# Where the second MLP's weight pairs are emitted beside the attention, and what their column sums are ordered behind

## The chip, the core and the metric

The kernel runs on one core of a Trainium2 chip. The metric is the time of one execution on the device, in microseconds (us), as the median of several runs. Beside it stands one execution recorded by the hardware profiler, whose trace gives every duration below.

Engines are named as the profile names them: PE is TensorE (matmuls), PEld its weight loads, DVE is VectorE, ACT is ScalarE, POOL is GpSimd, SP is SyncE, which issues nearly all DMAs here. Each engine works through its own list of instructions. A scheduler writes these lists when the program is built.

## The reference

```python
def _attn_ref(q, k, v, w1, b1, w2):                    # (4, 8, 576, 64) each
    scores = scale * np.matmul(q, k.transpose(0, 1, 3, 2))
    ...                                                # a bias per head from a small MLP on relative positions
    attn = np.exp(scores - max) / (sum + 1e-09)
    return np.matmul(attn, v)

def _moe_ref(x, w1, w2, w3, w_out):                    # first MLP: 2304 x 512, d_ff 768
    h = np.maximum(np.maximum(x @ w1, x @ w2), x @ w3)
    return h @ w_out

def _moe2_ref(x, w_in, w_out):                         # second MLP: 2304 x 512, d_ff 2048
    h = x @ w_in
    g = np.where(h >= 1, h, np.where(h <= -1, 0.0, (h + 1) ** 2 / 4))
    return g @ w_out
```

Attention, then the first MLP, then the second. Matrices are multiplied in two float16 parts, a high one and a low one, so each product takes three matmuls. Before a weight is split into these parts it is scaled by a power of two that is taken from the sums of its columns' sizes.

## The kernel before

**Attention.** The queries are cut into blocks `j` of 128 rows (and a last one of 64, `SJ`), and the work into slots: one slot is one head, or pair of heads, of one block and batch. The loop over `i` (line 939) emits, for slot `i`, its scores for the next slot, its softmax, side work, and the multiplication with V (`emit_pv`, 14 matmuls of 128x64, line 753, or 28 of line 749) of the slot three before. The first MLP's matmuls (line 808 with the three input weights, line 830 with the output weights) come from a queue `mlp_q`: some run beside the attention, and what is left is drained after the last slot by a loop over `mlp_q`.

**Weights of the second MLP.** `late_pieces` brings them in 16 pairs of 128 rows or columns of `w_in` and `w_out`. For a pair two raw tiles are loaded by SP (line 450) into buffers named `v` or `ws`. ACT and DVE decode them (lines 462, 463, 464, 465), then `pair_scale` takes the column sums: eight matmuls with a matrix of ones on PE (line 549, result in a PSUM tile `pm` or `s`), a maximum on DVE (line 552) and three small steps to the scale (lines 136, 137, 141), and ACT and DVE write the high and the low half (lines 157 and 158). `late_to(n)` emits pieces up to a number. In the attention's last blocks (`u.j >= 3`) it stops at `N_BIAS` = 10 pieces, that is five pairs; the other eleven pairs are emitted in the loop that drains `mlp_q`.

**The drain.** In it PE does the first MLP's matmuls of the last two groups of tokens, whose operands are named `masks` and `xT`, and the column sums of the eleven pairs. ACT decodes and splits weights, and takes the MLP's results out of PSUM (lines 813 and 835). DVE does its half of both.

**The second MLP, first block.** Per step `ft` PE multiplies with `w_in` (line 1056), ACT and DVE form the activation (ACT 1069, DVE 1070 and 1071, ACT 1073, DVE 1074), and PE multiplies with `w_out` two steps later (line 1082). Between these steps `wcomb(q)` is emitted eight times: POOL forms sums and differences of the weights that later blocks need (lines 1120 to 1124), ACT writes their high half (line 1125) and POOL the low one (line 1126). The other blocks (lines 1134 and 1173 on PE) follow.

**What sets the order.** The build's scheduler picks instructions by their priority and by a timeline of its own; `tc.issue_after(x)` keeps what is emitted inside it behind instruction `x` in the order. Without it an instruction can be put anywhere that its operands allow. So a small change in what is emitted when can reshuffle the lists further on.

Of the kernel before, what the change touches and what calls it, by code (L numbers as in the profile page):

```python
# [20 lines left out]
def kernel(ctx: ExitStack, tc: tile.TileContext, qt, kt, vr, small, mw1, mw2, mw3, mwo, win, wo2, out):  # L21
# [7 lines left out]
    V, A, G, T, SP = nc.vector, nc.scalar, nc.gpsimd, nc.tensor, nc.sync  # L29
    P = 128  # L30
# [46 lines left out]
    @contextmanager  # L77
    def sooner(what):

        n = PRM["po"].get(what, 0)  # L80
        n = min(n, tc.cur_priority)
        tc.cur_priority -= n
        yield
        tc.cur_priority += n
# [79 lines left out]
    if True:  # L164
# [303 lines left out]
        def high(y):  # L468

            return y.bitcast(BF16)[:, 0:512]  # L470
# [67 lines left out]
        def late_to(n):  # L538
            while n_late[0] < n:
                n_late[0] += 1  # L540
                next(late)

        def pair_scale(s, ys, k):

            pn = mlp_ps()
            for i, y in enumerate(ys):
                yb = high(y)
                for kk in range(KK):
                    T.matmul(pn[:, P * i:P * i + P], ones, yb[:, P * kk:P * kk + P], start=(kk == 0), stop=(kk == KK - 1))
            n = s.shape[1]  # L550
            t = st([P, 2], F32, "tcol2")[:, :n]
            V.tensor_reduce(t, pn[:, :2 * P].rearrange("p (n c) -> p n c", n=n), AX.X, ALU.max)
            floor2(t, t)
            inv2(s, t, k)
# [144 lines left out]
        def halves(t):  # L699
            return t.rearrange("p (a c) -> p a c", a=2)  # L700

        last_soft, last_turn = [None], [None]

        def emit_soft(i):
            u, s = slots[i]
# [32 lines left out]
        def emit_pv(i):  # L738
            u, s = slots[i]
            if s == 0:  # L740
                u.pav = ps.tile([P, 512], F32, tag="pav", name="pav", bufs=1)
            pt = ptbox.pop(i)
            for x, (c, sl) in enumerate(PVSEQ):
                kw = dict(start=(x == 0), stop=(x == len(PVSEQ) - 1))
                if u.j == SJ:
                    for r in range(2):
                        h = PAIRS[s][r]
                        v = kbox[("v", 3, u.b, h // 4)]
                        T.matmul(u.pav[64 * r:64 * r + 64, 64 * s:64 * s + 64], pt[:, c, 64 * r:64 * r + 64], v[:, sl, 64 * (h % 4):64 * (h % 4) + 64], **kw)
                else:  # L750
                    v = kbox[("v", u.j, u.b, s // 4)]
                    h = HEADS[s]
                    T.matmul(u.pav[:, 64 * h:64 * h + 64], pt[:, c], v[:, sl, 64 * (h % 4):64 * (h % 4) + 64], **kw)  # L753
            return s == u.n - 1

        xbox = {}
# [182 lines left out]
        for i in range(NS + LAG + 1):  # L939
            if i == NS:  # L940
                wide.append(1)
            if i < NS:
                u, s = slots[i]
                at = i - start_of[u.j]
                if at == 0 and u.j < 3:
                    with behind(i):
                        xts[u.j + 1] = xtable(u.j + 1)
                    bias_q.extend((u.j + 1, gq) for gq in range(18))
                    if u.j == 2:
                        xts[SJ] = xtable(SJ)  # L950
                        bias_q.extend((SJ, gq) for gq in range(9))
                with sooner("att"):
                    prefetch(i + PRM["ahead"])
                    prefetch_v(i)
                    emit_s(i + 1)
                    emit_soft(i)
            with sooner("norm"):
                while pend_norm:
                    emit_norm(pend_norm.pop(0))
            if i < NS:  # L960
                with sooner("v"):
                    if PRM["ef"]:
                        for f, *a in early.get(i, ()):
                            with behind(i), tc.issue_after(last_score[0].ins) if f is v_max else tc.issue_after(last_turn[0].ins) if f is v_store else nullcontext():
                                f(*a)
                with sooner("w"):
                    while conv_left and PRM["cm"][6 - len(conv_left)] <= i:
                        with behind(i):
                            conv_moe(conv_left.pop(0))
                b_at, b_n = PRM["bias"][min(u.j, 2)]  # L970
                with sooner("bias"):
                    for _ in range(rate("bias", (27 if u.j == 2 else 18) / b_n) if at >= b_at and not conv_left else 0):
                        if bias_q:
                            a = bias_q.pop(0)
                            a = (*a, new_xt(a[0]))
                            if a[0] == SJ:
                                bias_short(*a)
                            else:
                                bias_group(*a, B1[cnt["b"] % len(B1)])
                                cnt["b"] += 1  # L980
                with sooner("v"):
                    if not PRM["ef"]:
                        for f, *a in early.get(i, ()):
                            f(*a)
                if i >= (WO if n_wo[0] >= NF1 else PRM["woz"]):
                    with sooner("wo"):
                        for _ in range(rate("conv", PRM["c0"] if n_wo[0] < NF1 else PRM["c1"])):
                            if n_wo[0] != NF1 or i >= WO:
                                n_wo[0] += 1
                                next(pieces, None)  # L990
                with sooner("mlp"):
                    for _ in range(rate("mlp", PRM["mlp"][u.j])):
                        e = next_mlp(i >= WO and (wo_done or not PRM["ww"]))
                        if e:
                            e[0](*e[1])
            if i < NS and u.j >= 3:
                with sooner("late"), tc.issue_after(last_soft[0].ins):
                    late_to(min(N_BIAS, n_late[0] + rate("late", PRM["late"][0])))
            if i >= LAG and i - LAG < NS:
                with sooner("att"):  # L1000
                    last_pv = emit_pv(i - LAG)
                if last_pv:
                    uu = slots[i - LAG][0]
                    pend_norm.append(uu)
                    key = (uu.j, uu.b // 2 if uu.j != SJ else 0)
                    half = 4 * uu.j + uu.b < PRM["half"]
                    if half or uu.b == B - 1 or (uu.j != SJ and uu.b == 1):
                        done_blocks.append((i, key, slice(128 * (uu.b % 2), 128 * (uu.b % 2) + 128) if half else slice(0, 256)))
            while done_blocks and i >= done_blocks[0][0] + 2:
                queue_mlp(*done_blocks.pop(0)[1:])  # L1010
# [262 lines left out]
```

## Time and profile before

| | |
|---|---|
| median of 3 runs | 1004.85 us (1003.17, 1004.85, 1009.06) |
| profiled execution | 1001.5 us, span 999.6 us |
| PE busy | 927.2 us, 93% of the span |
| DVE, ACT, POOL busy | 689.0, 599.2, 514.1 us |
| mean granted TensorE clock | 0.96 of full speed |

The profiled execution has a time of its own, 1001.5 us; its span goes from the first to the last instruction. Busy times are sums over the whole span, so they hide that different stretches have different limits.

In the rows below a time is in us from the span's start, then comes the duration of a group, then engine, line, operation and operands (`out<-in`). What stands in square brackets is how long the engine had been idle before it, and whose end ended that.

### The profile page before, as it was taken

The numbers are of one execution on the slowest core, as the hardware profiler recorded it, in microseconds if no ns is written. First come the engines' busy times: TensorE is split into PE (matmuls) and PEld (weight loads), VectorE is DVE, ScalarE is ACT, GpSimd is POOL, SyncE is SP. The second block draws the span as 40 slices with busy tenths as digits, with TensorE's granted clock in tenths as the row PEclk, the third lists the DMA queues.
The fourth block names the chain that finished last, engine by engine and source line by source line (L and its number), as shares of the span: only waits on it lengthen the run. The fifth ranks groups of instructions, "written<-read, shape, count | busy, mean of one in ns | idle before, by whom it ended". The sixth has DMA issues, their size and how long they took to land. (4 is left out here: it accounts for less than half of the span.)

```text
span 999.6 us, 25925 instructions
## 1 busy us (share of the span) xinstructions
PE 927.2 (93%) x10258; PEld 756.0 (76%) x10258; DVE 689.0 (69%) x1512; ACT 599.2 (60%) x1194; POOL 514.1 (51%) x734
## 2 busy tenths in 40 slices
PE   6768988899999999999899899999999999999996
PEld 5546777688888878778678778543688888888885
DVE  8998886767656686566454577876477586686565
ACT  3789875856665645778577698633444454454442
POOL 4133496748767755646367103995143344343442
PEclk8777979899999999999999999999999999999999
DMA  9996997997999879999989663010110010000000
GB/s 289 266 261 161 271 220 210 232 247 168 218 237 206 178 178 212 218 230 225 216 172 210 193 202 106 22 43 1 43 44 23 1 43 23 2 22 23 1 23 22
DMA packets 238969, 141.46 MB, mean 142 GB/s; under 512 B 187520, under 2 KB 217728, under 8 KB 238336
## 3 DMA queue, kind: packets, MB, share of 16 engines
q1 hardware_dynamic: 238688, 139.55, 58.6%
q8 instruction: 80, 1.31, 0.5%
q14 instruction: 41, 0.34, 0.1%
q10 hardware_dynamic: 160, 0.26, 0.1%
HBM read 79.68 MB, written 15.27 MB: 95 GB/s over the span
## 5 line engine op out<-in xcount | busy, mean ns | idle before, releaser
L808 PEld LDWEIGHTS <-aw 128*128 128x128 f16 x2160 | 190.1, 99 | 42.5 <-issue 20.0
L808 PE MATMUL pm<-xT,aw 128*128 128x256 f16 (+1 forms) x1812 | 201.9, 264 | 4.4 <-ACT hl L835 2.0
L731 POOL TENSOR_TENSOR phl<-sp,phl 128x512 f16<-128x512 f32 x136 | 162.2, 1193 | 0.0
L713 ACT ACTIVATE sp<-sp,mx 128x576 f32<-128x576 f32 x144 | 110.6, 769 | 67.8 <-DVE mx L711 67.3
L730 POOL TENSOR_TENSOR phl<-sp,phl 128x64 f16<-128x64 f32 x136 | 49.0, 360 | 189.6 <-ACT phl L729 157.1
L697 PE MATMUL s<-k,qz 64*128 64x288 f32 (+1 forms) x576 | 127.1, 459 | 15.1 <-DVE mx L711 9.8
L711 DVE CUSTOM_DVE_ANT_0 sp<-s,ab 128x576 f32<-128x576 f32 x128 | 93.2, 751 | 28.0 <-PE s L697 13.8
L1151 ACT ACTIVATE sp<-pm,vec 128x256 f32<-128x256 f32 x112 | 61.3, 555 | 80.0 <-PE pm L1134 77.2
L697 PEld LDWEIGHTS s<-k,qz 64*128 64x128 f32 (+1 forms) x576 | 69.0, 199 | 33.7 <-DVE mx L711 12.5
L729 ACT ACTIVATE phl<-sp 128x576 f16<-128x576 f32 x136 | 90.0, 673 | 4.8 <-DMA pt<-phl 4.1
L753 PEld LDWEIGHTS <-pt 128*128 128x128 f16 x1792 | 72.3, 100 | 25.5 <-DMA pt<-phl 14.4
L1155 POOL TENSOR_TENSOR hh<-hh 128x128 f32<-128x128 f32 x56 | 32.9, 588 | 106.4 <-DVE hh L1153 90.3
L1134 PEld LDWEIGHTS <-ab 128*128 128x128 f16 x756 | 73.8, 98 | 9.2
L753 PE MATMUL pav<-v,pt 128*128 128x64 f16 x1568 | 69.2, 195 | 9.0 <-DMA pt<-phl 8.9
L1152 DVE SCALAR_TENSOR_TENSOR hh<-pm,vec,sp 128x256 f32<-128x256 f32 x112 | 52.4, 477 | 32.3 <-ACT sp L1151 32.0
L820 POOL TENSOR_TENSOR hh<-hm,hh 128x256 f16<-128x256 f32 (+1 forms) x60 | 45.9, 766 | 52.4 <-ACT hh L819 52.3
L830 PE MATMUL pm<-hh,wo 128*128 128x256 f16 x558 | 70.3, 276 | 1.7 <-ACT hh L819 0.9
L830 PEld LDWEIGHTS <-wo 128*128 128x128 f16 x648 | 61.6, 99 | 13.1 <-issue 5.0
L815 DVE SCALAR_TENSOR_TENSOR hm<-pm,hm 128x256 f32<-128x256 f32 (+1 forms) x108 | 42.0, 389 | 33.7 <-PE pm L808 16.3
L1173 PEld LDWEIGHTS <-xT 128*128 128x128 f16 x588 | 57.4, 98 | 7.8 <-ACT xT L1160 1.2
L1173 PEld LDWEIGHTS <-wo 128*128 128x128 f16 x588 | 57.5, 98 | 6.7
L1156 POOL TENSOR_TENSOR hh<-hh 128x128 f32<-128x128 f32 x56 | 26.2, 468 | 68.4 <-DVE hh L1153 66.2
(298 smaller groups left out, 1986.1 us busy)
## 6 DMA issues: line engine op xcount, KB each, us to landing
k<-in_k_dram SPq DMA_DIRECT2D x64, 288.0 KB, 4.0
v<-v_d SPq DMA_DIRECT2D x24, 640.0 KB, 5.0
ws<-in_moe_w_out_dram SPq DMA_DIRECT2D x15, 512.0 KB, 5.1
ws<-in_moe_w_in_dram SPq DMA_DIRECT2D x9, 512.0 KB, 5.9
x_d<-hl SPq DMA_DIRECT2D x36, 128.0 KB, 2.6
qz<-in_q_dram SPq DMA_DIRECT2D x16, 256.0 KB, 4.4
ab<-in_moe_w_dram SPq DMA_DIRECT2D x8, 512.0 KB, 8.6
qz<-x_d SPq DMA_DIRECT2D x4, 1024.0 KB, 4.8
```

The lines of the kernel that those rows point to most:

```text
L697: last_score[0] = T.matmul(sbox[i + r][:, c, :288], q[p, s if u.j == SJ else s // 2], k[p, 288 * c:288 * c + 288], start=True, stop=True)
L711: last_pair[0] = V.tensor_tensor_reduce(halves(sn), sbox.pop(i)[:, :, :288], halves(bias_sb[u.j][:, h]), -0.125, 3e38, ALU.add, ALU.min, mx)
L713: last_soft[0] = A.activation(pf, sn, AF.Exp, scale=-1.0, bias=mx, accum_out=u.sums[:, h:h + 1])
L729: A.activation(hl[:, :S], pf, AF.Copy)
L731: G.tensor_tensor(hl[:, S + 64:], pf[:, :512], hl[:, :512], ALU.subtract)
L753: T.matmul(u.pav[:, 64 * h:64 * h + 64], pt[:, c], v[:, sl, 64 * (h % 4):64 * (h % 4) + 64], **kw)
L808: T.matmul(o, wm[:, ft, i, wp, kk], x_rhs(key, xp, kk) if n == 256 else x_rhs(key, xp, kk)[:, c], start=(x == 0), stop=(x == 11))
L830: T.matmul(pm, wo16[:, ft, wp, P * d:P * d + P], hh[:, ft, hp], start=(ft == 0 and y == 0), stop=(ft == NF1 - 1 and y == 2))
L1134: T.matmul(pm, w[:, wp, kk], x2t[ORDER[y]][:, kk, xp, 256 * sub:256 * sub + 256], start=(x == 0), stop=(x == 11))
L1151: A.activation(r, pm, AF.Relu, scale=c_ch[:, f], bias=c_half)
L1152: V.scalar_tensor_tensor(t, pm, c_c[:, f], r, ALU.mult, ALU.max)
L1173: T.matmul(m[x], gl[:, gp, i], w[:, wp], start=(start and z == 0 and x % 2 == 0), stop=(stop and z == 2 and (x % 2 == 1 or x == 6)))
```

## The change

The call of `late_to` inside the attention moves: it stood ahead of `emit_pv`, and stands behind it now. It is under the same condition and with the same number, as `i >= LAG` always holds there. And the eight column-sum matmuls of each pair are put into `tc.issue_after(last_mm)`, where `last_mm` is the last multiplication with V that was emitted. The softmax order that it was under (`last_soft`) stays. After the attention `last_mm` remains the very last multiplication with V, so the column sums of the drain's eleven pairs are ordered behind that one too.

```diff
@@ pair_scale
             pn = mlp_ps()
-            for i, y in enumerate(ys):
-                yb = high(y)
-                for kk in range(KK):
-                    T.matmul(pn[:, P * i:P * i + P], ones, yb[:, P * kk:P * kk + P], start=(kk == 0), stop=(kk == KK - 1))
+            with tc.issue_after(last_mm[0].ins) if last_mm else nullcontext():
+                for i, y in enumerate(ys):
+                    yb = high(y)
+                    for kk in range(KK):
+                        T.matmul(pn[:, P * i:P * i + P], ones, yb[:, P * kk:P * kk + P], start=(kk == 0), stop=(kk == KK - 1))
@@ emit_pv (both matmuls)
-                    T.matmul(u.pav[:, 64 * h:64 * h + 64], pt[:, c], ...)
+                    last_mm[:] = [T.matmul(u.pav[:, 64 * h:64 * h + 64], pt[:, c], ...)]
@@ the slot loop
-            if i < NS and u.j >= 3:
-                with sooner("late"), tc.issue_after(last_soft[0].ins):
-                    late_to(min(N_BIAS, n_late[0] + rate("late", PRM["late"][0])))
             if i >= LAG and i - LAG < NS:
                 with sooner("att"):
                     last_pv = emit_pv(i - LAG)
+                if i < NS and u.j >= 3:
+                    with tc.issue_after(last_soft[0].ins):
+                        late_to(min(N_BIAS, n_late[0] + rate("late", PRM["late"][0])))
```

The diff adds one line, so from `pair_scale` on most line numbers of the changed kernel are one higher: its column sums are line 550, the multiplication with V 754, the first MLP 809, its evictions 814 and 836, `wcomb`'s ACT step 1126.

In the built programs the lists of all five engines have the same instructions in the same order, line numbers aside, up to the last slot of the attention. The five pairs beside the attention stand where they stood. The first place that differs is on PE, in the last slot: the column sums of the first pair of the drain (operands `xtab` and `ab`) beside the last 14 multiplications with V. Before:

```order
L808 MATMUL s<-masks,aw 128x256
L549 LDWEIGHTS ones
L549 MATMUL s<-xtab,ones 128x128
L549 LDWEIGHTS ones
L549 MATMUL s<-xtab,ones 128x128
L753 LDWEIGHTS pt
L753 MATMUL pav<-v,pt 128x64
```

And the same place in the changed kernel:

```order
L809 MATMUL s<-masks,aw 128x256
L809 LDWEIGHTS aw
L809 MATMUL pm<-masks,aw 128x256
L754 LDWEIGHTS pt
L754 MATMUL pav<-v,pt 128x64
...
L550 LDWEIGHTS ones
L550 MATMUL s<-xtab,ones 128x128
```

Two of the eight column sums stood ahead of the 14 multiplications and six behind; now all eight stand behind, and two first-MLP matmuls have moved ahead in their place.

Further on, in the drain, ACT's list is dealt out differently. The names: `hl` is the first MLP's output taken out of PSUM (tiles `pm`, `s`), `masks`, `ws` and `ab` are places of weights. Before, in the middle of the drain:

```order
L835 ACTIVATE hl<-pm,vec 128x64 x4
L835 ACTIVATE hl<-s,vec 128x64 x4
L462 ACTIVATE sp<-v 128x512
L463 ACTIVATE ws<-ws 128x512
L462 ACTIVATE sp<-ws 128x512
L463 ACTIVATE ws<-v 128x512
L835 ACTIVATE hl<-pm,vec 128x64 x4
L465 ACTIVATE ws<-sp 128x512
L835 ACTIVATE hl<-pm,vec 128x64 x2
L157 ACTIVATE masks<-sp,vec 128x512 x2
L835 ACTIVATE hl<-pm,vec 128x64 x2
```

Now:

```order
L462 ACTIVATE sp<-v 128x512
L836 ACTIVATE hl<-pm,vec 128x64 x4
L836 ACTIVATE hl<-s,vec 128x64 x4
L463 ACTIVATE ws<-v 128x512
L465 ACTIVATE ws<-sp 128x512
L462 ACTIVATE sp<-ws 128x512
L463 ACTIVATE ws<-ws 128x512
L157 ACTIVATE masks<-sp,vec 128x512 x2
L463 ACTIVATE ws<-v 128x512
L836 ACTIVATE hl<-pm,vec 128x64 x4
L814 ACTIVATE hm<-s 128x256
L836 ACTIVATE hl<-pm,vec 128x64 x4
```

The third and the fourth eviction of the group (`hl<-pm`) now stand behind more weight work: one L465, the two L157 and one L463 have moved ahead of the third.

The last place is ACT's list at the start of the second MLP. Before:

```order
L1125 ACTIVATE aw<-xT 128x1024
L835 ACTIVATE hl<-s,vec 128x128 x2
L1069 ACTIVATE sp<-pm,vec 128x512
L1073 ACTIVATE phl<-sp,vec 128x512
L1069 ACTIVATE sp<-pm,vec 128x512
L1125 ACTIVATE aw<-xT 128x1024
L835 ACTIVATE hl<-s,vec 128x128 x2
L835 ACTIVATE hl<-pm,vec 128x128 x2
L1073 ACTIVATE phl<-sp,vec 128x512
L1069 ACTIVATE sp<-pm,vec 128x512
```

Now:

```order
L1126 ACTIVATE aw<-xT 128x1024
L836 ACTIVATE hl<-s,vec 128x128 x2
L1070 ACTIVATE sp<-pm,vec 128x512
L1074 ACTIVATE phl<-sp,vec 128x512
L1126 ACTIVATE aw<-xT 128x1024
L836 ACTIVATE hl<-s,vec 128x128 x2
L836 ACTIVATE hl<-pm,vec 128x128 x2
L1070 ACTIVATE sp<-pm,vec 128x512
L836 ACTIVATE hl<-s,vec 128x128 x2
L1070 ACTIVATE sp<-pm,vec 128x512
L1074 ACTIVATE phl<-sp,vec 128x512 x2
L1126 ACTIVATE aw<-xT 128x1024
```

The second activation step (the second L1069, now L1070) stood ahead of the second `wcomb` step and stands behind it. Further on three more pairs of neighbours change places: the fourth L1069 stood ahead of the third `wcomb` step and stands behind it, the eighth L1069 stood ahead of the sixth `wcomb` step and stands behind it, and the ninth L1073 stood ahead of the seventh and stands behind it. The eighth and last `wcomb` step stands between the tenth L1073 and the eleventh L1069 in both.

## Rows read from the trace of the kernel before

**Rows 1.** Busy us (and instructions) of each engine by stretch; clock, DMA share, GB/s

```profile
0.00:545.00 545.00, 492.10 (x6578) 405.22 (x6579) 383.88 (x914) 372.50 (x816) 321.07 (x441) 0.93 0.96 219
545.00:632.00 87.00, 79.17 (x784) 67.91 (x782) 57.88 (x142) 67.05 (x141) 21.33 (x24) 1.00 0.52 162
632.00:693.00 61.00, 57.42 (x273) 25.94 (x272) 43.78 (x46) 26.14 (x39) 56.65 (x47) 1.00 0.07 24
693.00:962.00 269.00, 269.00 (x2363) 230.97 (x2364) 184.07 (x376) 122.30 (x184) 103.76 (x201) 1.00 0.06 22
```

**Rows 2.** The chain that ended last, around the start of the second MLP

```profile
622.61 2.70 DVE k L158 x2
...
628.68 2.42 POOL aw L1126
...
688.53 0.77 ACT sp L1069
...
692.17 0.76 DVE phl L1074
692.98 2.33 PE s L1082 x10
```

**Rows 3.** PE in order of time, in the drain

```profile
572.76 0.38 PE L549 MATMUL pm<-ab,ones 128*128 128x128 bf16 x4 [1.30 <-ACT ab L465]
...
595.56 1.47 PE L808 MATMUL pm<-xT,aw 128*128 128x256 f16 x12
598.06 1.47 PE L808 MATMUL pm<-xT,aw 128*128 128x256 f16 x12 [1.03 <-ACT hl L835]
...
607.48 2.78 PE L808 MATMUL s<-xT,aw 128*128 128x256 f16 x24 [1.81 <-ACT hm L813]
```

**Rows 4.** ACT in order of time, drain and start of the second MLP

```profile
574.93 0.68 ACT L463 ACTIVATE ab<-v 128x512 uint32<-128x512 uint32 x1 [1.71 <-DMA v<-in_moe_w_out_dram]
...
594.51 0.94 ACT L835 ACTIVATE hl<-pm,vec 128x64 f32<-128x64 f32 x4
...
596.21 1.39 ACT L157 ACTIVATE masks<-sp,vec 128x512 f16<-128x512 f32 x2
...
604.44 0.67 ACT L463 ACTIVATE k<-v 128x512 uint32<-128x512 uint32 x1 [0.91 <-DMA v<-in_moe_w_out_dram]
...
632.32 0.76 ACT L1069 ACTIVATE sp<-pm,vec 128x512 f32<-128x512 f32 x1
...
637.80 0.63 ACT L835 ACTIVATE hl<-pm,vec 128x128 f32<-128x128 f32 x2
...
644.87 1.06 ACT L1125 ACTIVATE aw<-xT 128x1024 f16<-128x1024 f32 x1 [2.11 <-POOL xT L1124]
...
671.98 1.06 ACT L1125 ACTIVATE aw<-xT 128x1024 f16<-128x1024 f32 x1 [3.71 <-POOL xT L1124]
...
680.50 1.06 ACT L1125 ACTIVATE aw<-xT 128x1024 f16<-128x1024 f32 x1 [2.11 <-POOL xT L1124]
```

**Rows 5.** PE in order of time, first block of the second MLP

```profile
638.84 1.89 PE L1082 MATMUL s<-ab,phl 128*128 128x512 f16 x8
...
669.18 2.33 PE L1082 MATMUL s<-ab,phl 128*128 128x512 f16 x10 [0.70 <-DVE phl L1074]
...
675.87 2.33 PE L1082 MATMUL s<-ab,phl 128*128 128x512 f16 x10 [1.34 <-DVE phl L1074]
...
680.63 2.75 PE L1082 MATMUL s<-ab,phl 128*128 128x512 f16 x12
...
692.19 0.60 PE L1082 MATMUL s<-ws,phl 128*128 128x512 f16 x2 [1.04 <-ACT phl L1073]
```

**Rows 6.** POOL in order of time, `wcomb`: one step in two lengths

```profile
632.20 0.73 POOL L1122 TENSOR_TENSOR xT<-xT 128x256 f32<-128x256 f32 x1
...
667.40 1.17 POOL L1122 TENSOR_TENSOR xT<-xT 128x256 f32<-128x256 f32 x1
```

**Rows 7.** DVE in order of time, the same stretch: L1074 beside POOL

```profile
655.43 2.46 DVE L1074 SCALAR_TENSOR_TENSOR phl<-sp,vec,phl 128x512 f16<-128x512 f32 x1 [1.19 <-ACT phl L1073]
```

More of the change, by code (lines that the diff above doesn't have):

```diff
@@ L700, in halves @@
             return t.rearrange("p (a c) -> p a c", a=2)
-        last_soft, last_turn = [None], [None]
+        last_soft, last_turn, last_mm = [None], [None], []
         def emit_soft(i):
@@ L748, in emit_pv @@
                         v = kbox[("v", 3, u.b, h // 4)]
-                        T.matmul(u.pav[64 * r:64 * r + 64, 64 * s:64 * s + 64], pt[:, c, 64 * r:64 * r + 64], v[:, sl, 64 * (h % 4):64 * (h % 4) + 64], **kw)
+                        last_mm[:] = [T.matmul(u.pav[64 * r:64 * r + 64, 64 * s:64 * s + 64], pt[:, c, 64 * r:64 * r + 64], v[:, sl, 64 * (h % 4):64 * (h % 4) + 64], **kw)]
                 else:
@@ L752, in emit_pv @@
                     h = HEADS[s]
-                    T.matmul(u.pav[:, 64 * h:64 * h + 64], pt[:, c], v[:, sl, 64 * (h % 4):64 * (h % 4) + 64], **kw)
+                    last_mm[:] = [T.matmul(u.pav[:, 64 * h:64 * h + 64], pt[:, c], v[:, sl, 64 * (h % 4):64 * (h % 4) + 64], **kw)]
             return s == u.n - 1
```

## The prediction

> **What bounds the kernel now.** I read the busy times by stretch first, then the chain of waits, then PE and ACT in order of time where the chain changes engine.
>
> The stretches [rows 1] tell where a change could matter at all. From 693 to 962 us PE is busy 269.00 of 269.00 us. Nothing that only moves instructions can shorten that. From 545 to 632, the drain of the first MLP, PE is busy 79.17 of 87.00 us and ACT 67.05. From 632 to 693, the first block of the second MLP, PE is busy 57.42 of 61.00 us and POOL 56.65. So PE is idle 7.83 us in the drain and 3.58 us in the block behind it, 11.41 us together. The granted clock is 1.00 in all three stretches, the full 2.4 GHz level, although PE waits in two of them, so I count no clock loss and no gain.
>
> The chain [rows 2] says which engine sets the end of the second stretch. It runs through DVE's last weight pairs (622.61), then along POOL's `wcomb` from 628.68 to the eighth step, then to ACT's L1069 at 688.53, DVE's L1074 at 692.17 and PE's L1082 at 692.98, and from there along PE to the end. So the end comes when POOL's chain and what is behind it is through, and PE has some room until then: its waits at 669.18, 675.87 and 692.19 [rows 5].
>
> **The attention: 0.** No instruction is added or removed. The five pairs beside the attention are the first 10 of 32 pieces. On all five lists they stand where they stood, so emitting them later in the slot, and behind the multiplication with V, changes nothing in the first 545 us [rows 1]. With equal lists the waits are equal too. What is left is the drain and the block behind it.
>
> **The last slot: 0.** Two column sums move behind the 14 multiplications with V. These are eight short matmuls; four of them take 0.38 us as a group [rows 3]. Nobody waits for them there: the next steps of that pair on DVE stand behind a decode step that waits for a DMA.
>
> **The drain, ACT's first part: 0, from -1.3 to 0.** An eviction and a decode step change places around 562 us. Whatever PE gains there it loses at 572.76, where it waits 1.30 us for ACT's L465 [rows 3], which is as late as before, since the same ACT steps stand in front of it. If ACT came earlier by all of that wait, 1.30 us would be won.
>
> **The drain, the first MLP's evictions: 0, up to +1.5.** The third eviction of the group, at 594.51 before, now has one L465, two L157 and one L463 more in front of it. By rows the two L157 take 1.39 us and an L463 0.67 [rows 4]; taking the same for an L465 this makes 2.7 us, so the eviction starts at about 597.2 and ends at 598.1 with its 0.94. PE's twelve matmuls that ran at 595.56 need its PSUM buffer [rows 3]. They come 2.5 us late. The wait of 1.03 us at 598.06 for the fourth eviction then falls away, because the fourth now follows directly and PE arrives later: 1.5 us are left. At 607.48 PE waited 1.81 us for ACT [rows 3], and that swallows the 1.5. I take 0, and keep +1.5 for the case that the ACT step waited for there comes later as well.
>
> **The drain, the loads: 0, from -2.6 to +0.7.** SP's list differs in a handful of loads of weights that move by a place ahead of or behind stores of the first MLP's output. ACT waited 1.71 us for a landing at 574.93 and 0.91 at 604.44 [rows 4], together 2.62. Where ACT frees raw buffers earlier, the next load starts earlier. Around 604 I read a gain of some 0.6 from the order: two L462 that free raw tiles stand earlier by about that. But soon behind it the two L157 of another pair, which took 1.39 in the row above, have moved behind an L463 that waits for a load, so that ACT waits with work left to do, and gives it back. Hence 0.
>
> **The start of POOL's chain: 0.** The gate is the last pair's scale, behind DVE's two L158 at 622.61 [rows 2]; the order around it on DVE, and the L157 and the first L1125 on ACT behind it, are as before but for one L819.
>
> **The first block of the second MLP: +1.2.** Here ACT's list puts activation steps behind `wcomb` steps that wait for POOL. Four cases:
>
> - The second L1069 was at 632.32. Now it is behind the second L1125 and four evictions, which ended at 637.80 + 0.63 = 638.4 [rows 4]. From an L1069 to its L1074's end it takes 4.4 us on the chain (688.53 to 692.93) [rows 2], and one more activation step of about 0.8 stands between now: ready at 643.6. PE's second L1082 group would start after the first one, which began at 638.84 [rows 5] and takes 2.6, at about 641.5. PE is 2 us late, and its later waits of 0.70 and 1.34 [rows 5] swallow that.
> - The third L1125, at 644.87 [rows 4], now follows the third L1073. The second step's result is there at 643.6, and about 2 us of DVE's and ACT's work for the third follow: 645.6, which is 0.7 later. POOL had other work in most of that time, so I let its chain lose 0.2.
> - The eighth L1069 now stands behind the sixth L1125, which ends at 671.98 + 1.06 = 673.0 [rows 4]. With 4.4 us its result is there at 677.4. PE took it up at 675.87 [rows 5]: +1.5.
> - The ninth L1073 stands behind the seventh L1125, so it starts at 680.50 + 1.06 = 681.6 [rows 4], and with L1073 and L1074 of about 0.75 each the result is there at 683.1. PE began that group at 680.63 [rows 5], and would now begin at 682.1, so it loses another 0.9: +2.4 in all.
>
> At 692.19 PE waited 1.04 and then 0.18 us more, until 692.98, for the eleventh step [rows 2, 5], which still depends on POOL's eighth `wcomb`. That swallows 1.2 of the 2.4. So +1.2 is left, and POOL's 0.2 lies beside it. From 693 on PE has no idle time, so +1.2 goes to the end in full. Bounds: 0, if the waits are dealt out more kindly, and +2.4.
>
> One more price in this stretch is POOL's. Its L1122 takes 0.73 us at 632.20 and 1.17 at 667.40 [rows 6], and DVE's L1074, 0.76 on the chain at 692.17 [rows 2], takes 2.46 us at 655.43 [rows 7], next to POOL. So the two engines hold each other up when they meet, and the change moves DVE's steps against POOL's. I take 0 for it, as the number of meetings is about the same.
>
> **Sum.** 0 + 0 + 0 + 0 + 0 + 1.2 = +1.2 us on the profiled execution's own time of 1001.5, that is 1002.7. That execution is 3.35 us below the median of the three runs (1004.85), which themselves range over 5.9 us. The mean of all four executions is 1004.6. I put the sum on that: 1004.6 + 1.2 = 1005.8.
>
> **Rivals.**
>
> 1. *The drain gets shorter.* If earlier freed raw buffers take both waits for landings (1.71 + 0.91) from ACT [rows 4] and PE follows, POOL's chain starts 2.6 us earlier and PE's losses behind it stay: 1004.6 - 2.6 + 1.2 = 1003.2; without those losses 1002.0. For a gain of over 5 us nearly half of the 11.41 us would have to go. For it speaks that ACT has little other idle time in the drain; against it that the order gives back at the next pair what it wins.
> 2. *POOL's chain gets longer* (slower). If the activation's DVE steps now meet `wcomb` at other points, each of eight L1122 could take 1.17 in place of 0.73, which is +3.5, and the 1.2 of PE's waits turn into POOL's. From the point where the eighth L1125 ends later than before, each microsecond goes straight to the end, as PE waits for it at 692.19. With the late third L1125 and the +1.5 of the evictions: 1004.6 + 3.5 + 0.2 + 1.5 = 1009.8.
>    The Trainium skill's page "SBUF — State Buffer", section "SBUF: two separate sides", says that VectorE and GpSimd share one pair of ports as an exclusive lock, and that the one which comes second waits for the other's whole instruction. By that rule, the trace agrees: 2.46 is 0.76 and most of another engine's instruction. A `wcomb` step could then lose a whole 0.76 per meeting, eight times 6.1, and the sum would be 1010.7.
> 3. *The change does what its words say in the attention after all*, that is the same lists run in another rhythm. Then the five pairs' forty column sums come later, at 0.38 us per four: 3.8 us of PE work shifted, of which the end would see at most 3.8 in either direction, 1000.8 or 1008.4. Against it speaks that nothing on the lists differs.
>
> **How the numbers follow.** Forecast 0.66, rival 1 0.16, rival 2 0.14, rival 3 0.04. The forecast's own range is 1003 to 1008: its bounds 0 to +2.4 and half of the scatter of the runs. With rivals 1 and 2 and half of the scatter below the former's 1002.0 to 1003.2 the range is 1000 to 1010. What differs by less than 0.5%, 5 us, a measurement of this kernel can't tell from no change. Over 5 us faster needs rival 1 with more than its waits, 0.06 of its 0.16, and 0.02 from the forecast and rival 3: 0.08. Slower by over 5 us is over half of rival 2 (0.08) and a little of the forecast and rival 3 (0.02): 0.10. Same is the rest: 0.82.
>
> **What would show it right or wrong.** In the new profile: the attention up to the last slot with the times of before to a few tenths; a PE wait near 595 that is longer, and the one near 607 shorter or gone; the eighth `wcomb` step on ACT near 688; waits of PE for L1074's results near 642, 676 and 682, and none or a short one at 692. The idle time of PE between 545 and 693 should be 12 to 14 us where it was 11.41. I am wrong if the eighth `wcomb` step comes more than 2 us earlier or later, or if the attention's times move.

## The result, and the profile after

The changed kernel takes 1012.73 us in the median of 11 runs (1010.16 to 1018.76), the kernel before 1007.84 in 11 runs beside it (1002.31 to 1009.93). The ratio is 1.0065, with a 95% interval of 1.0046 to 1.0085. So the change makes the kernel slower by 0.65%; the medians lie 4.9 us apart, the means 6.6. I had forecast no measurable change, 1005.8 us in a range of 1000 to 1010: the forecast was wrong.

The profiled execution took 1011.35 us, with a span of 1009.6. First its busy times by stretch, in the columns of [rows 1]:

```profile
0.00:545.00 545.00, 488.56 (x6551) 402.05 (x6552) 379.62 (x911) 369.01 (x811) 319.97 (x438) 0.93 0.97 217
545.00:632.00 87.00, 75.86 (x785) 66.91 (x782) 55.88 (x132) 66.38 (x139) 18.20 (x25) 1.00 0.56 170
632.00:693.00 61.00, 55.34 (x258) 25.20 (x257) 44.82 (x56) 26.07 (x40) 56.06 (x46) 0.97 0.08 27
693.00:962.00 269.00, 269.00 (x2321) 226.66 (x2319) 181.42 (x366) 121.11 (x181) 103.06 (x197) 1.00 0.06 21
```

PE's idle time from 545 to 693 is 11.14 + 5.66 = 16.80 us, where it was 11.41. I had expected 12 to 14. The granted clock, 1.00 before, is 0.97 in the third stretch.

The two profiles can't be laid on each other as they are. The last multiplication with V begins at 554.89 us before and at 557.63 after, though the instructions ahead of it are the same; over the 13 profiles of this study that I could use it lies between 554.89 and 565.41. So I take its start as the zero, and compare what comes behind, which I call the tail. First before, then after:

```profile
554.89 0.57 PE L753 MATMUL pav<-v,pt 128*128 128x64 f16 x14
```

```profile
557.63 0.57 PE L754 MATMUL pav<-v,pt 128*128 128x64 f16 x14
```

By that measure the kernel before ends at 999.6 - 554.89 = 444.7 us and the changed one at 1009.6 - 557.63 = 452.0: 7.3 more.

PE in order of time, answering to [rows 3, 5]:

```profile
595.71 1.47 PE L809 MATMUL pm<-xT,aw 128*128 128x256 f16 x12 [0.32 <-ACT hl L836]
...
601.94 1.47 PE L809 MATMUL pm<-xT,aw 128*128 128x256 f16 x12 [2.14 <-ACT hl L836]
...
612.17 2.78 PE L809 MATMUL s<-xT,aw 128*128 128x256 f16 x24 [1.31 <-ACT hm L814]
...
645.42 2.02 PE L1083 MATMUL s<-ab,phl 128*128 128x512 f16 x6 [2.90 <-ACT hl L836]
647.24 3.91 PE L1057 MATMUL pm<-ws,ab 128*128 128x512 f16 x12
...
692.20 2.33 PE L1083 MATMUL s<-ab,phl 128*128 128x512 f16 x10 [1.35 <-DVE phl L1075]
```

The wait for the third eviction is there, 2.14 us. The matmuls of 595.56 in [rows 3] are at 601.94, and with 2.74 us taken off for the zero that is 3.6 later. The wait of 1.03 is gone, but that of 1.81 us [rows 3] has only fallen to 1.31, so 612.17 - 607.48 - 2.74 = 1.95 us of lateness pass it. The first L1083 is 3.8 us late, behind a wait of 2.90, and the twelve L1057 behind it take 3.91 us, where twelve matmuls of that size took 2.75 before [rows 5]: the clock has fallen after the wait. From 646 to 648 us the granted clock is 0.54, from 648 to 650 it is 0.61.

The chain of waits, answering to [rows 2]. It runs along POOL again, then DVE and PE:

```profile
636.89 2.15 POOL aw L1127
...
687.11 1.18 POOL xT L1125
690.01 2.14 DVE phl L1075
692.20 2.33 PE s L1083 x10
```

And ACT's steps in it, first those of the kernel before, the first and the eighth:

```profile
627.56 1.04 ACT L1125 ACTIVATE aw<-xT 128x1024 f16<-128x1024 f32 x1
...
687.57 1.06 ACT L1125 ACTIVATE wo<-xT 128x1024 f16<-128x1024 f32 x1 [2.48 <-POOL xT L1124]
```

Then the changed kernel:

```profile
634.53 1.33 ACT L157 ACTIVATE k<-sp,vec 128x512 f16<-128x512 f32 x2 [4.92 <-DVE vec L141]
635.77 1.04 ACT L1126 ACTIVATE aw<-xT 128x1024 f16<-128x1024 f32 x1
...
688.31 1.06 ACT L1126 ACTIVATE aw<-xT 128x1024 f16<-128x1024 f32 x1 [3.26 <-POOL xT L1125]
689.27 0.70 ACT L1074 ACTIVATE phl<-sp,vec 128x512 f16<-128x512 f32 x1
...
695.40 1.06 ACT L1126 ACTIVATE wo<-xT 128x1024 f16<-128x1024 f32 x1 [0.67 <-POOL xT L1125]
```

ACT stood 4.92 us in front of the last pair's L157, waiting for its scale from DVE. The first `wcomb` step follows at 635.77. It was at 627.56, so with 2.74 taken off for the zero it is 8.2 - 2.74 = 5.5 us late. The eighth, at 695.40, was at 687.57: 5.1 late. The chain is thus not longer than before, it starts later. And PE's last wait now ends behind the seventh step (688.31), not the eighth.

### The profile page after: what moved, and what is told of

It is laid out like the page before. It is cut to its first block, busy times and chain, and to the rows that moved or that the text cites. A ratio compares the mean times of both kernels' runs of the same rounds, so it can differ in the third digit from the quotient of the medians.

```text
span 1009.6 us, 25929 instructions
## 1 busy us (share of the span) xinstructions
PE 927.8 (92%) x10258; PEld 755.3 (75%) x10258; DVE 689.0 (68%) x1512; ACT 599.0 (59%) x1194; POOL 512.9 (51%) x734
## 3 DMA queue, kind: packets, MB, share of 16 engines
q8 instruction: 80, 1.31, 0.5%
## 5 line engine op out<-in xcount | busy, mean ns | idle before, releaser
L714 ACT ACTIVATE sp<-sp,mx 128x576 f32<-128x576 f32 x144 | 110.5, 768 | 66.7 <-DVE mx L712 66.3
```

Of the source, the lines that this page charges most:

```text
L714: last_soft[0] = A.activation(pf, sn, AF.Exp, scale=-1.0, bias=mx, accum_out=u.sums[:, h:h + 1])
```

## Experiments

For all profiles this table has the start of the last multiplication with V, and counted from there the first `wcomb` step on ACT (in e5, e6, e10 and e11 it isn't on ACT), the eighth low half on POOL (L1126 before), and the span's end, that is the tail; the last column is the end less the eighth step.

| kernel | last V | first step | eighth | end | end - eighth |
|---|---|---|---|---|---|
| before | 554.89 | 72.7 | 133.8 | 444.7 | 310.9 |
| e1 changed, drain not ordered | 560.00 | 74.3 | 135.1 | 446.0 | 310.9 |
| e4 before, scales behind | 565.41 | 73.0 | 134.7 | 445.6 | 310.9 |
| changed | 557.63 | 78.1 | 138.9 | 452.0 | 313.1 |
| e2 order alone | 561.85 | 77.4 | 138.1 | 451.3 | 313.1 |
| e3 changed, scales behind | 560.56 | 75.6 | 136.4 | 449.4 | 313.0 |
| e9 changed, eviction first | 561.26 | 76.9 | 138.4 | 449.5 | 311.1 |
| e8 both | 562.00 | 73.5 | 135.1 | 446.2 | 311.1 |
| e12 both, again | 562.58 | 74.5 | 136.1 | 447.3 | 311.2 |
| e5 before, copies on POOL | 560.79 | - | - | 440.7 | - |
| e11 the same, again | 562.94 | - | - | 441.4 | - |
| e6 changed, copies on POOL | 560.06 | - | - | 444.8 | - |
| e10 the same, eviction first | 556.82 | - | - | 443.5 | - |

### Which part of the change it is: e1 and e2

```diff
 e1 (changed kernel)
         fetch_x2(0)
+        last_mm.clear()
         for x, (f, a) in enumerate(mlp_q):
```

e2 is the kernel before with `issue_after(last_mm)` around the column sums, and `late_to` left where it was. Line numbers aside, e1's lists of all five engines are those of the kernel before, and e2's are those of the changed one.

> The changed kernel in full, except that the column sums of the drain's pairs are no longer ordered behind anything: the note of the last matmul with V is forgotten before the first MLP is drained. The pairs emitted in the attention keep both parts of the change. Theory (only the drain's first pair has its sums moved, and all that was lost follows from that): the time of the kernel before, ratio 0.998 to 1.002, with POOL's first L1127 near 629 us and last L1083 near 721 us. Rival A (the sums ordered behind the matmuls with V, or the pairs emitted at the end of a slot, cost time inside the attention): stays near the changed kernel, ratio 1.004 to 1.009, and the first column sum near 409 us again.

> The ordering alone: the pairs are emitted where the kernel before emits them, but every pair's column sums are ordered behind the last matmul with V. Theory: the changed kernel's time, ratio 1.005 to 1.009, first L1126 of POOL's chain about 5 us later than before when the last matmul with V is taken as the zero. Rival A (the position of the pairs' emission costs): between the two kernels, ratio 1.001 to 1.004.

e1: ratio 1.0016 (0.9992 to 1.0040). e2: 1.0065 (1.0040 to 1.0089). So the position of the pairs beside the attention costs nothing, and neither does their order there, nor the `sooner("late")` that the moved call lost. The whole loss comes from the drain, and there from the first pair's sums, two of which moved behind 14 multiplications with V: with the order on that pair alone the lists are those of the changed kernel, too, and with it on every pair but that one they are those of the kernel before. The absolute times that I wrote for e1 were missed, because its attention was 5 us slower; in the table it stands with the kernel before.

### VectorE's scale steps: e3 and e4

```diff
                     if ft % GROUP == 0:
-                        scales(0, slice(ft, ft + GROUP), ft // GROUP)
+                        with tc.issue_after(last_split[0].ins):      # the last pair's L158
+                            scales(0, slice(ft, ft + GROUP), ft // GROUP)
```

In the changed kernel, as in the kernel before, DVE's list has four scale steps for the second MLP between the second last pair's scale (L141) and its split (L158). In the changed kernel:

```profile
627.75 0.44 DVE L141 TENSOR_SCALAR vec<-tcol 128x2 uint32<-128x2 uint32 x1
628.22 0.65 DVE L1033 TENSOR_SCALAR vec<-vec 128x16 f32<-128x16 f32 x1
628.91 0.60 DVE L141 TENSOR_SCALAR vec<-vec 128x16 uint32<-128x16 uint32 x1
629.54 1.07 DVE L1035 TENSOR_SCALAR vec<-vec 128x16 f32<-128x16 f32 x1
630.53 0.77 DVE L1036 TENSOR_SCALAR vec<-vec 128x16 f32<-128x16 f32 x1
631.22 2.30 DVE L158 SCALAR_TENSOR_TENSOR k<-sp,vec,k 128x512 f16<-128x512 f32 x2
```

Before, with the same four steps between them:

```profile
620.39 0.15 DVE L141 TENSOR_SCALAR vec<-tcol 128x2 uint32<-128x2 uint32 x1
...
622.52 2.78 DVE L158 SCALAR_TENSOR_TENSOR k<-sp,vec,k 128x512 f16<-128x512 f32 x2
```

The last pair's scale is behind all of them. The edit changes DVE's list alone.

> The changed kernel, with DVE's scale steps of the second MLP's first block (four rows of VectorE's list) put behind the split of the last pair of weights; no other engine's list differs. Theory (the last pair's scale waits on VectorE behind these steps, which take about 3 us beside POOL's first group, and POOL's chain of L1126 and L1127 follows one to one): the split of the last pair 2 to 3 us earlier, first L1126 and the end 2 to 3 us earlier, ratio 1.002 to 1.006 to the kernel before. Rival B (the chain of wcomb groups does not set the end; TensorE's matmuls in the drain do): the split comes earlier, the end does not move, ratio 1.005 to 1.009. Rival C (the scale steps are then late for the first group of the second MLP): the end moves by less than 1 us or gets later.

> The kernel before with the same edit of VectorE's list alone. Theory: there the last pair's scale is held by these steps for about 1 us, so the split comes up to 1 us earlier and the end with it, ratio 0.998 to 1.0. Rival B: nothing moves, ratio 0.999 to 1.001. Rival C: the scale steps are late for the first group, ratio 1.001 to 1.003.

e3: ratio 1.0036 (1.0012 to 1.0060). DVE, with the steps behind the last pair's split:

```profile
630.11 0.44 DVE L141 TENSOR_SCALAR vec<-tcol 128x2 uint32<-128x2 uint32 x1
631.40 2.55 DVE L158 SCALAR_TENSOR_TENSOR k<-sp,vec,k 128x512 f16<-128x512 f32 x2 [0.85 <-ACT k L157]
...
635.72 1.41 DVE L158 SCALAR_TENSOR_TENSOR k<-sp,vec,k 128x512 f16<-128x512 f32 x2 [0.87 <-ACT k L157]
...
637.52 1.98 DVE L1037 TENSOR_SCALAR vec<-vec 128x16 f32<-128x16 f32 x1
```

From L141 to the first L158 it takes 1.29 us where it took 3.47. In the table the first step of the chain is 1.8 to 2.5 us earlier than in the two profiles of the changed lists, and the end 1.8 to 2.5 earlier. That is the theory, at the lower end of the size expected, and it speaks against rival B, though the interval of the ratio still overlaps that of the change. It doesn't make these steps the cause of the loss. They stand in the same place in the kernel before, where L141 to L158 took 2.13 us, and in e1, which has that kernel's lists, 3.77, more than the changed kernel's 3.47. So e3 takes out a price that both kernels pay.

e4: ratio 1.0035 (1.0009 to 1.0060), above all that I wrote, rival C's 1.001 to 1.003 included. But the profile doesn't show rival C: the end is 445.6 us behind the last V, as in the other two kernels with the lists of before, so in the tail nothing moved (rival B). There the split did come earlier, but ACT then waited 0.84 us for POOL's own sums:

```profile
636.26 1.33 ACT L157 ACTIVATE k<-sp,vec 128x512 f16<-128x512 f32 x2 [2.26 <-DVE vec L141]
638.43 1.06 ACT L1127 ACTIVATE aw<-xT 128x1024 f16<-128x1024 f32 x1 [0.84 <-POOL xT L1126]
```

What is late next took the place of the wait. In this profile what e4 loses lies ahead of the last multiplication with V, which began at 565.41; the last section comes back to it.

### Does POOL's chain carry the loss to the end: e5, e6 and e11

```diff
-            A.activation(t_home[q][:, 0], t, AF.Copy)      # ACT, L1125
+            G.tensor_copy(t_home[q][:, 0], t)              # POOL
```

The lists differ from those of the two kernels only from the first such copy on.

> The kernel before, with the eight copies of POOL's chain (ScalarE's L1125, float32 to float16) done on POOL itself, so that ScalarE's list holds no step that waits for POOL between the steps that release TensorE. The chain gets longer by what eight such copies take on POOL, but the first reader of its result is the second block. Theory (the chain sets the end because its steps stand in ScalarE's list): the waits of TensorE in the first block (1.34 us at 675.87, 1.04 us at 692.19) go, the end comes 2 to 4 us earlier, ratio 0.996 to 0.998. Rival B (TensorE's own work and its waits in the drain set the end): nothing moves, 0.999 to 1.001. Rival C (POOL, fuller by the copies, slows VectorE's steps or is late for the second block): slower, 1.002 to 1.01.

> The changed kernel with the same edit. Theory: here the chain starts about 5 us later and holds TensorE longer, so the edit gives back more, 5 to 7 us; what is left against the same edit of the kernel before is TensorE's own lateness in the drain, 2 to 3 us. Ratio to the kernel before 0.998 to 1.001. Rival B: ratio stays at 1.005 to 1.009, and the difference to the other kernel with this edit stays 5 to 7 us. Rival C: slower than the changed kernel.

> The kernel before with the copies on POOL, the fastest so far, beside the same kernel's runs once more. Theory (the chain's steps in ScalarE's list cost the kernel before its two waits in the first block, 3.5 us in all): ratio 0.996 to 0.999. Rival (that gain is lost to POOL and VectorE in each other's way): 1.0 to 1.002.

e5: 0.9991 (0.9971 to 1.0011), and measured again as e11 0.9946 (0.9923 to 0.9969). e6: 0.9995 (0.9973 to 1.0017), where the changed kernel had 1.0065. With the copies off ACT's list the changed kernel is back at the time of the kernel before, and not at rival B's 1.005 to 1.009. For the kernel before the times alone don't decide: e5's ratio fits rival B's 0.999 to 1.001, e11's lies below all that I wrote. The tails and the waits do. POOL, which has 9.35 us of idle time behind the chain in e5, isn't late for the second block (rival C). This is the whole list of what PE waited for from 555 to 760 us in e5 (us in total, times, longest):

```profile
PE s L808 <- ACT hm L813: 2.5, 2, 1.8
PE pm L808 <- ACT hl L835: 2.0, 2, 1.0
PE pm L549 <- ACT ab L465: 1.3, 1, 1.3
PE pav L753 <- DMA pt<-phl: 1.0, 1, 1.0
PE s L549 <- ACT ab L465: 0.8, 1, 0.8
PE s L549 <- ACT hl L835: 0.2, 1, 0.2
```

No line of the first block is left in it. In the kernel before two more stood there, and in the changed kernel three. First before:

```profile
PE s L1082 <- DVE phl L1074: 2.5, 4, 1.3
...
PE s L1082 <- ACT phl L1073: 1.0, 1, 1.0
```

Then the changed kernel:

```profile
PE s L1083 <- ACT hl L836: 2.9, 1, 2.9
...
PE s L1083 <- DVE phl L1075: 1.8, 2, 1.3
...
PE s L1083 <- ACT phl L1074: 0.9, 1, 0.9
```

By the table the edit takes 3.3 to 5.3 us from the three kernels with the lists of before, and 6.4 to 7.1 from the two with the changed ones. e6 still ends 3.5 to 4.1 us behind e5 and e11. A part of that is the clock of this one execution. In the columns of [rows 1], e6:

```profile
605.00:620.00 15.00, 15.00 (x136) 12.88 (x134) 9.55 (x24) 12.22 (x26) 1.34 (x2) 0.89 0.49 158
```

Behind a wait of 2.09 us for the eviction the granted clock fell to 0.50, the 1.2 GHz level, and two groups of twelve matmuls took 1.91 and 2.74 us, where such a group took 1.47 before [rows 3]: 1.7 us more. In e5 and e11 it stayed at 1.00 from 545 to 693. By that estimate 1.8 to 2.4 us are left for TensorE's own lateness in the drain, about the 2 to 3 expected. So the chain carries a part of the loss, and hides the rest as long as it is later than TensorE.

### The eviction that TensorE waits for: e7, e9, e8, e12 and e10

```diff
                 for i in range(2):
-                    split(dst[i][:, 0:512], dst[i][:, 512:1024], zs[i], ...)
+                    with tc.issue_after(last_ev[0].ins) if last_ev and y == 10 else nullcontext():
+                        split(dst[i][:, 0:512], dst[i][:, 512:1024], zs[i], ...)
```

Here `last_ev` is the newest eviction (L836) of the first MLP's last block, and `y == 10` the pair whose two L157 on `masks` had moved ahead of it. The edit moves more than this pair: the lists of PE, ACT and DVE differ from the changed kernel's in further places of the drain and the first block, those of POOL and SP don't. e8 and e12 have e3's edit as well, e10 has e6's.

> The changed kernel with the split of the sixth pair's first half (ScalarE's two L157 on masks, 1.3 us) ordered behind the eviction of the first MLP that TensorE waits for at 601.94 (2.14 us); the scheduler moves some other steps of the drain with it. Theory (evictions that stand behind decoding work in ScalarE's list hold TensorE, and the lateness goes on to the last pair and POOL's chain): the 2.14 us wait falls to about 0.8 us, the last first-MLP matmul and POOL's first step come 1 to 2 us earlier, ratio 1.003 to 1.006. Rival D (the drain's lateness comes from the loads and decodes of the last pairs, which the evictions don't touch): the wait falls, POOL's first step and the end stay, 1.005 to 1.008.

> The changed kernel with the eviction put first, once more, for its profile. Theory (the eviction's wait goes on to POOL's chain): last matmul with V to the span's end 1 to 2 us shorter than the changed kernel's 452.0, first step of POOL's chain 1 to 2 us earlier, ratio 1.003 to 1.006. Rival D (the eviction's wait is made up or handed on to other waits of the drain): 451 to 452.5, ratio 1.005 to 1.008.

> The changed kernel with the eviction put first and with VectorE's scale steps put behind the last pair's split. Theory: both gains add, POOL's first step 3.5 to 4.5 us earlier than in the changed kernel, ratio 1.0 to 1.003. Rival D: as with the scale steps alone, 1.003 to 1.005.

> The changed kernel with both edits of the drain, once more, since its profile stood at the level of the kernel before (446.2 us from the last matmul with V to the end) and its times did not. Theory (nothing but the drain and the order of POOL's chain differs, so the tail decides): 445 to 447 us in the profile again, ratio 0.999 to 1.002. Rival (something outside the tail costs 2 to 3 us in this kernel, in each run): 445 to 447 us in the profile, ratio 1.003 to 1.005, with the last matmul with V later than 560.

> The changed kernel with the eviction put first and with the copies of POOL's chain done on POOL. Without the chain in ScalarE's list the drain's waits of TensorE are the only ones left, so they count in full. Theory (part of the drain's lateness is the eviction's wait): 1 to 2 us shorter than the changed kernel with the copies on POOL alone, ratio 0.997 to 0.999. Rival D: the same as that kernel, 0.999 to 1.001.

e7: 1.0056 (1.0033 to 1.0079), which fits the theory's range and rival D's alike. Its profiled execution took 1542.53 us at a granted clock of 0.554, so I read no tail from it. e9, the same kernel: 1.0029 (1.0004 to 1.0054), just below the theory's range. Its end is 449.5 us behind the last V, 1.7 to 2.4 less than with the changed lists. But it isn't the wait that went: PE waited 1.92 us in that place, because an L463 ahead of the eviction waited 0.97 us for a load. The first step is only 0.5 to 1.3 us earlier, the eighth between 0.5 earlier and 0.3 later, and 2.0 us come from the last column of the table, which fell from 313.1 to 311.1. For the scheduler had also put the seventh and eighth step elsewhere on ACT:

```profile
688.64 0.72 ACT L1079 ACTIVATE phl<-sp,vec 128x512 f16<-128x512 f32 x1 [3.35 <-DVE sp L1077]
691.47 1.06 ACT L1131 ACTIVATE aw<-xT 128x1024 f16<-128x1024 f32 x1 [2.10 <-POOL xT L1130]
...
695.34 0.72 ACT L1079 ACTIVATE phl<-sp,vec 128x512 f16<-128x512 f32 x1 [2.14 <-DVE sp L1077]
698.54 1.06 ACT L1131 ACTIVATE wo<-xT 128x1024 f16<-128x1024 f32 x1 [2.48 <-POOL xT L1130]
```

Here the step that makes `phl` (L1079) stands ahead of the seventh `wcomb` step (691.47). In the changed kernel it stood behind it (689.27 behind 688.31), and PE waited there. So the theory's number was met by luck, through a mechanism that it didn't name.

e8: 1.0039 (1.0014 to 1.0063); e12, the same kernel: 1.0019 (0.9997 to 1.0042). The first step is at 73.5 and 74.5, in the kernel before and e1 at 72.7 and 74.3. The end is at 446.2 and 447.3, where those two have 444.7 and 446.0. So with both edits the tail is back to within 1.4 us of before on the mean (446.8 and 445.4), though e12's lies just above the 445 to 447 that I wrote, and though e3's part of the edit takes out steps that the kernel before pays for as well. The ratios are less clear: e12's lies in the theory's range, e8's in rival D's. On the mean they are 1.003, about 2.9 us, where the tails differ by 1.4; whether something ahead of the tail costs the rest stays open. e10: 0.9970 (0.9948 to 0.9993), the low end of the theory, with a tail of 443.5, 1.4 less than e6. But e6 lost 1.7 us by the clock and e10 nothing (1.00 from 545 to 693), and the intervals of the two ratios overlap. So e10 doesn't show that the eviction's wait counts.

The fastest kernel is the one of e5 and e11. The intervals of its two ratios just fail to overlap (0.9971 and 0.9969), its two tails lie 0.7 us apart and 3.3 to 5.3 below those with the lists of before.

## Why the prediction was wrong

- **The base, 1004.6.** I put the sum on the mean of four executions; beside the changed kernel the one before took 1007.84. Of the 6.9 us between 1005.8 and 1012.73 this makes 3.2. The other 3.7 are the change's own, 4.9 in place of 1.2. To a loss of over 5 us, which the means show, I had given 0.10.
- **The attention, 0; the last slot, 0.** Right. Equal lists cost nothing (e1), and the profiled attention's 2.7 us are scatter: e1, with the lists of before, has 5.1.
- **ACT's first part, 0.** Right to 0.1 us: the sums of 572.76 came at 575.41, which is 572.67 with 2.74 taken off.
- **The clock, no loss.** It did fall in the first block, and the twelve L1057 took 1.2 us longer for it. The tail doesn't show it: in e3 the clock stayed at 1.00, and its last column in the table is 313.0, the changed kernel's 313.1. PE's later waits took it up: at 684.44 it waited 0.85 us, in e3 2.07 in the same place.
- **The evictions, 0 up to +1.5.** Mis-sized. The lateness was 3.6 us and not 2.5, and the wait that was to swallow it gave only 0.5 (1.81 to 1.31): 1.95 remained. The ACT step waited for there was itself late. I had named that case and taken it at 0 in the sum.
- **The loads, 0.** The L463 of 604.44 [rows 4] came at 607.85 behind a wait of 1.05 us, which makes 0.7 us late, the upper end that I gave. But the term stopped there: the next three that waited for a landing, at 610.63, 615.45 and 617.61 in the changed kernel, were at 606.51, 611.66 and 613.12, so they are 1.4, 1.1 and 1.8 us late. This term is mis-sized too.
- **"The start of POOL's chain: 0."** This is the step that failed. I looked at the order around the gate, found it as before, and concluded that the start is as before. But an unchanged order only hands on the lateness of its inputs. The first step came 5.5 us later against the one profile of before, and 4.3 on the mean of two profiles each (77.8 and 73.5). Nearly all of that is there ahead of the gate. The second last pair's scale on DVE (L141, at 620.39 and 627.75) comes 65.5 us behind the zero in the kernel before and 70.1 in the changed one. Over the five profiles with the drain's lists of before it lies at 65.5 to 66.3, over the four with the changed ones (e6 among them) at 69.4 to 70.1: 3.9 later on the mean. The scale steps behind it add little to that: in e5 and e11 they took 2.1 us as in the kernel before, in e1 3.77, in the changed kernel, e2 and e6 3.5. With the order of e7's edit (e8, e9, e10, e12) the scale comes at 67.2 to 68.8, 1.6 us earlier on the mean than with the changed lists. That the single eviction carries this isn't shown, since e9 didn't shorten its wait, and what carries the other 2.3 stays open. The loads are a rival that no run tests alone: the chain that the profile follows back runs in the drain through two loads of raw weights, which take 3.63 and 3.63 us in it before, 5.96 and 4.87 in the changed kernel.
- **POOL's chain itself, 0.** Right: from the first to the eighth step on ACT 59.6 us, before 60.0. Rival 2 fails by this; rival 1 fails as the drain got longer, rival 3 as equal lists gave equal times.
- **The first block, +1.2.** Right in place, the seventh step against `phl`; measured 313.1 - 310.9 = 2.2 us, inside its bounds of 0 to 2.4 and nearly twice the sum's term. The wait of 2.90 us for an eviction at 645.42 was not among my four cases.

So the loss is about 4.3 us from the start of the chain and 2.2 from its steps' places on ACT, 6.5 together; the tails' means differ by 451.6 - 445.4 = 6.2, the means of the runs by 6.6 and their medians by 4.9. My sum had the second term only. The prediction's sign to look for, that the eighth step comes over 2 us later, is what the profile shows.

## What to carry to other kernels

Where a chain of waits sets the end, follow its first link back to its inputs and carry their lateness on; that the order at the gate is unchanged says nothing. A constraint on two small matmuls can cost more than they take, for the scheduler deals out all that comes after anew: compare the lists first, and test the ordering apart from the rest. And a step that waits for a slow engine in the list of an engine that feeds TensorE makes the slow chain critical; moving it into the slow engine's own list took the chain off the path. Last, an edit that wins time doesn't show that what it took out caused the loss: look whether the faster kernel has it too, as with e3's scale steps.

## What the runs showed of the hardware

The granted clock of the first 150 us differs between executions of the same instructions there. e1 and e4 have the same lists up to the drain. First e1, then e4, in the columns of [rows 1]:

```profile
50.00:100.00 50.00, 33.82 (x295) 24.11 (x295) 44.11 (x96) 45.88 (x88) 17.94 (x25) 0.79 0.82 215
100.00:150.00 50.00, 43.21 (x650) 35.69 (x649) 43.29 (x92) 39.80 (x86) 34.59 (x41) 0.90 1.09 242
```

```profile
50.00:100.00 50.00, 39.04 (x292) 28.50 (x291) 40.00 (x88) 43.55 (x83) 15.31 (x22) 0.66 0.77 194
100.00:150.00 50.00, 46.06 (x568) 37.01 (x569) 39.24 (x89) 40.11 (x83) 30.89 (x39) 0.76 1.08 255
```

With 0.66 and 0.76 of 2.4 GHz where the other had 0.79 and 0.90, PE was through 860 matmuls and not 945, and the last multiplication with V came 5.4 us later. Scatter of this size is as large as the effect. A straight line through the 251 runs of e1 to e12 and of the kernel before beside them that took under 1050 us, with a level for each kernel and chip, gives about 2.9 us less for 0.01 more of the mean granted clock. It doesn't explain all: e4's ratio over its 12 runs is 1.0035, though its tail is that of before, and what its runs lost ahead of the tail I can't say from one profile.

The clock also fell behind waits of PE in the tail, in four of the 13 profiles: in the changed kernel behind 2.90 us (3.91 us for twelve matmuls in place of 2.75), in e2 behind 2.09 and 2.07, in e9 behind 3.11 and in e6 behind 2.09. It doesn't follow each such wait: behind the 2.14 us at 601.94 in the changed kernel twelve matmuls took 1.47 us as before, and e3 had 1.00 throughout with a wait of 2.07. So the same lists can lose a further 1.7 us in one execution and nothing in another.

POOL's copy of 128x1024 values from float32 to float16 took 1.09 us on average in e5, about as long as ACT's 1.06 [rows 4], while its subtraction with an output of that size took 2.51. And DVE's steps on 128x16 values, 0.17 us where POOL is quiet (697.63 in the kernel before), took from 0.16 up to 1.98 us beside POOL's chain, so a handful of them is worth a place in a sum.
